# Small matmuls behind the scores of the first half of the first attention, and a shorter emission of the second attention

## The chip, the cores and the metric

The kernel runs on one core of a Trainium2 chip. Its time is the device time of one execution in microseconds; the times shown are those of several runs, and one further execution was recorded by the hardware profiler. TensorE (PE) does the matmuls, VectorE (DVE) and ScalarE (ACT) work on the results, GpSimd (POOL) does a part of the preparation and issues some DMAs, SyncE (SP) issues most DMAs.

## The reference

Four batches of twelve heads of attention over 448 tokens with normalized queries and keys, then two feed-forward layers over all 1792 tokens:

```python
q_n, k_n = (rmsnorm(q, g_q), rmsnorm(k, g_k))          # (4, 12, 448, 64)
scores = scale * np.matmul(q_n, k_n.transpose(0, 1, 3, 2))
attn = np.exp(scores - np.max(scores, axis=-1, keepdims=True))
attn = attn / (np.sum(attn, axis=-1, keepdims=True) + 1e-09)
x = np.matmul(attn, v)                                 # as (1792, 768)
h = x @ w_in                                           # (768, 2048)
y = (h * (1.0 / (1.0 + np.exp(-1.702 * h)))) @ w_out   # (2048, 768)
h = y @ w_in2
out = (np.maximum(h, 0.0) + alpha * np.minimum(h, 0.0)) @ w_out2
```

## The kernel before, in words

**Batches and units.** The work goes batch by batch: the attention of batch b + 1 runs beside the first layer of batch b, and the second layer comes last. A batch has six pairs of heads (NP = 6), and a pair has four units (UNITS): a unit is one set of query columns of both heads, and units 0 and 1 of a pair make up its first half, columns 0 to 256. So unit u belongs to pair u // 4, and batch 0 has the units below 4 * NP = 24.

**The first attention.** Batch 0 is computed in 32-bit floats: scores by two matmuls in the source (four instructions in the profile, line 509), probabilities transposed by TensorE (line 599) and copied by ScalarE (line 604), the sums of exponentials spread by TensorE (line 565), and then the values (line 639). It runs in two passes. `first_pairs` goes through units 0 and 1 of all six pairs, while the words of w_in become 16-bit halves on ScalarE and VectorE (lines 148, 164, 165, 179, 180, 245); three steps of that preparation are emitted per attention step. The second pass goes through units 2 and 3, with the preparation of w_out and the first half of batch 0's hidden units (`first_in`, line 743) beside it. During these stretches POOL loads the values of later batches to scale them (lines 312, 313).

**A unit's scores.** `scores` takes a PSUM tile sp of two banks of 512 columns, of which two buffers exist. It writes columns 0 to 448 of each bank, and VectorE reads the maxima out of them (line 523). `exponent` has ScalarE compute the exponentials out of sp (line 542), after which the buffer is free. `attention` emits, for step i, the scores and exponentials of unit i, the transposes of unit i - 2 (`low`), and the values of the units four steps back (five, from batch 1 on). From batch 1 on the scores are 16-bit matmuls (line 518), and the probabilities are transposed by DMAs on SP's queue (lines 618, 623) before the values.

**The first layer.** For batch 0, `first_moe1` emits the hidden units of columns 256 to 448 in 32 steps (16 blocks, two steps each; line 743, then lines 751 and 752 and the split into halves, lines 140 and 141), and `moe1_out` emits six output columns j in four steps each (line 806, 48 matmuls each, stored by SP, line 815). TICKS = 56 is the sum of both. For the other batches `moe1` takes the place of the hidden part (line 783).

**What sets the order.** Instructions are emitted in program order; a planner with a simulated timeline then orders them on each engine, earlier emitted ones first where several are ready. Every engine works off its queue in that order. At the end of `attention_moe_kernel` the loop over batches emits step i of a batch's first layer, and then as many steps of the next batch's attention as are due by then:

```python
lead = 0 if b else B1_AT
want = first + (last - first) * min(1.0, max(0.0, i + 1 - lead) / (PACE[b] * TICKS - lead))
```

B1_AT = 24 and PACE was 1.0 for all batches. For batch 0 the attention steps 24 to 52, 29 of them, are so spread over 32 steps of the first layer: the last eight steps of the hidden units and the 24 of the output columns. `ones` and `ident` are 128x128 constants of 16 bits (bf16); `tc.issue_after(ins)` orders what is emitted inside it behind `ins` on the same engine.

Of the kernel before, what the change touches and what calls it, by code (L numbers as in the profile page):

```python
# [24 lines left out]
VLAG = 0  # L25
LAG_ = 4
LAG2 = 5
PACE = (1.0, 1.0, 1.0, 1.0)
HOLD = 12800
M_AT = 2  # L30
VS_AT = 8
# [26 lines left out]
def attention_moe_kernel(  # L58
# [17 lines left out]
    nc = tc.nc  # L76
    B, H, S, D = q.shape
# [4 lines left out]
    NP = H // 2  # L82
# [15 lines left out]
    ident = const.tile([128, 128], BF16, name="ident")  # L98
    ones = const.tile([128, 128], BF16, name="ones")
# [395 lines left out]
    def unit(u):  # L495

        P, r = divmod(u, 4)
        return (P, *UNITS[r])

    def scores(u):  # L500
        P, _, _, place = unit(u)
        t1, _ = preps[P]
        sp = ps_s.tile([128, 2, 512], F32, tag="s", name="sp")
        n = 1 if place == 3 else 2
        if u < 4 * NP:
            q0 = (place - 4) * 128 if n == 2 else ST
            for j in range(2):
                ds = slice(64 * j, 64 * j + 64)
                nc.tensor.matmul(
                    out=sp[:, j, 0:S] if n == 2 else sp[ds, 0, 0:S], lhsT=t1[ds, 1, q0:q0 + 64 * n], rhs=t1[ds, 0],  # L510
                    start=True, stop=True
                )
        for i, (e, f) in enumerate(((0, 0), (0, 1), (1, 0)) if u >= 4 * NP else ()):
            kt = t1[:, NT2 * f:NT2 * f + 4].rearrange("p c t -> p (c t)")
            qt = t1[:, NT2 * e + place]
            for j in range(2):
                ds = slice(64 * j, 64 * j + 64)
                nc.tensor.matmul(  # L518
                    out=sp[:, j, 0:S] if n == 2 else sp[ds, 0, 0:S], lhsT=qt[ds] if n == 2 else qt[ds, 64:128], rhs=kt[ds, 0:S],
                    start=(i == 0), stop=(i == 2)  # L520
                )
        nm = small.tile([128, 2], F32, tag="nm", name="nm")
        nc.vector.tensor_reduce(out=nm[:, 0:n], in_=sp[:, 0:n, 0:S], op=ALU.max, axis=AX, negate=True)  # L523
        if u >= 4 * NP:
            nc.scalar.activation(out=nm[:, 0:n], in_=nm[:, 0:n], func=AF.Copy, scale=c_s)  # L525
        probs[u] = (sp, nm, n)
# [151 lines left out]
    def attention(us):  # L678

        LAG = LAG_ if us[0] < 4 * NP else LAG2  # L680
        for i in range(len(us) + LAG):
            if 0 < i <= len(us):
                high(us[i - 1])
            if i < len(us):
                scores(us[i])
                exponent(us[i])
            late = us[0] >= 4 * NP
            for what in (1, 0) if late else (0, 1):
                if what == 0 and 2 <= i <= len(us) + 1:
                    low(us[i - 2])  # L690
                if what and i >= LAG and us[i - LAG] % 2 == 1:
                    values(us[i - LAG] // 4, us[i - LAG] % 4 // 2)
            yield
# [470 lines left out]
    if True:  # L1164
# [80 lines left out]
        for b in range(B):  # L1245
            last = min(NU, 4 * NP * (b + 2)) + LAG2
            first = done
            got = None
            for i, _ in enumerate(moe1(b) if b else first_moe1(g0)):
                lead = 0 if b else B1_AT  # L1250
                want = first + (last - first) * min(1.0, max(0.0, i + 1 - lead) / (PACE[b] * TICKS - lead))
                while done < min(want, NU + LAG2):
# [37 lines left out]
```

## Time and profile before

| what | us |
|---|---|
| median of 3 runs (1151.21 to 1152.9) | 1152.63 |
| the profiled execution | 1150.06 |
| its span, first to last instruction | 1148.2 |
| PE busy | 1059.5 (92%) |
| DVE busy | 803.6 (70%) |
| ACT busy | 680.9 (59%) |
| POOL busy | 177.7 (15%) |
| mean granted clock of TensorE | 0.970 |

The shares are means over stages with different limits, so each stage is to be read by itself. A busy share of TensorE counts matmuls that are being worked on, at whichever clock is granted. The granted clock is a share of full speed: 1.00 is 2.4 GHz and 0.50 is 1.2 GHz, and a value between them says that a stretch had both. A wait names what came last for the instruction that waited.

### The profile page before, as it was taken

How to read it: one execution, taken by the hardware profiler on the slowest of the kernel's cores; microseconds unless marked ns; L12 is line 12 of the kernel's file. 1: busy time of each engine (PE TensorE's matmuls, PEld its weight loads, DVE VectorE, ACT ScalarE, POOL GpSimd, SP SyncE). 2: the span in 40 equal slices, each digit the busy share in tenths (PEclk: the TensorE clock that was granted, in tenths of full speed). 3: DMA queues.
4: the chain of work that ended last, by engine and by line, in shares of the span. 5: the costliest groups of instructions: out<-in, count | busy, mean ns of one | idle time of the engine just before them, and what ended most of it. 6: DMA issues, size and time to landing. Idle time of an engine off the chain costs nothing.

```text
span 1148.2 us, 18347 instructions
## 1 busy us (share of the span) xinstructions
PE 1059.5 (92%) x6752; PEld 580.6 (51%) x6752; DVE 803.6 (70%) x1390; ACT 680.9 (59%) x1396; POOL 177.7 (15%) x364
## 2 busy tenths in 40 slices
PE   3676898897989999999999999999999999999998
PEld 1343566644434555555455455444444477666664
DVE  6988899987869874577533956599977223968341
ACT  4788786878878976688633562356555324645220
POOL 2722003765433242100000000000000000000000
PEclk9687999999989999999999999999999999999999
DMA  7984553478887656555446601665442323363111
GB/s 224 280 212 140 163 153 94 98 165 186 188 164 144 149 135 141 114 118 114 79 117 224 220 1 64 234 219 188 153 157 74 137 70 113 101 188 102 33 30 28
DMA packets 235562, 158.25 MB, mean 138 GB/s; under 512 B 167888, under 2 KB 214736, under 8 KB 235472
## 3 DMA queue, kind: packets, MB, share of 16 engines
q1 hardware_dynamic: 229200, 141.41, 44.4%
q0 software_dynamic: 6272, 15.67, 5.5%
q8 instruction: 53, 0.87, 0.3%
q14 instruction: 37, 0.30, 0.1%
HBM read 92.41 MB, written 25.69 MB: 103 GB/s over the span
## 4 chain that ended last, share of the span: by engine, by line
PE 58%; DVE 14%; DMA 10%; issue 8%; ACT 5%; POOL 4%; SPq 1%; ACTq 0%; DVEq 0%; POOLq 0%
PE op L1072 16%; PE yp L806 14%; PE hp L783 11%; PE h L912 10%; PE xp L639 3%; PE sp L518 2%; DMA pt<-ph 1%; DMA t<-hl 1%; DMA qk<-in_q_dram 1%; DVE ph L611 1%; DMA g<-in_moe_w_out_dram 1%; DMA w2raw<-in_moe_w_in_dram 1%; DVE w2num L165 1%; ACT pr L542 1%; DVE g L141 1%
## 5 line engine op out<-in xcount | busy, mean ns | idle before, releaser
L806 PE MATMUL yp<-g,w1o 128*128 128x448 f16 x1152 | 225.7, 354 | 0.0
L912 PE MATMUL h<-x,w2i 128*128 128x512 f16 (+1 forms) x1152 | 218.9, 352 | 3.1 <-DVE pos L918 1.7
L783 PE MATMUL hp<-x,w1i 128*128 128x448 f16 x864 | 170.4, 354 | 0.9 <-DVE t L792 0.9
L912 PEld LDWEIGHTS <-w2i 128*128 128x128 f16 x1152 | 112.7, 98 | 108.5 <-issue 3.9
L806 PEld LDWEIGHTS <-w1o 128*128 128x128 f16 x1152 | 110.0, 98 | 108.4 <-issue 8.6
L783 PEld LDWEIGHTS <-w1i 128*128 128x128 f16 x864 | 82.0, 98 | 83.4 <-issue 9.8
L523 DVE TENSOR_REDUCE nm<-sp 128x2 f32<-128x896 f32 x96 | 92.7, 966 | 12.6 <-PE sp L518 11.9
L611 DVE SCALAR_TENSOR_TENSOR ph<-pr,sm,ph 128x448 f16<-128x448 f32 x126 | 86.9, 723 | 19.2 <-ACT ph L584 19.1
L917 ACT ACTIVATE pos<-h,sign 128x512 f32<-128x512 f32 (+1 forms) x64 | 40.1, 628 | 86.6 <-PE h L912 80.4
L542 ACT ACTIVATE pr<-sp,nm,c_s 128x448 f32<-128x448 f32 x126 | 90.0, 717 | 2.3 <-DVE ph L611 0.9
L1072 PEld LDWEIGHTS <-even 128*128 128x128 f16 x672 | 65.7, 98 | 43.4
L918 DVE SCALAR_TENSOR_TENSOR pos<-h,slope,pos 128x512 f32<-128x512 f32 (+1 forms) x64 | 43.6, 683 | 60.0 <-ACT pos L917 60.0
L584 ACT ACTIVATE ph<-pr,sm 128x448 f16<-128x448 f32 x126 | 77.5, 658 | 12.3 <-DVE sm L581 11.8
L743 PE MATMUL hp<-x,w1i 128*128 128x256 f16 (+1 forms) x576 | 61.1, 263 | 9.4 <-DVE g L752 7.0
L1072 PEld LDWEIGHTS <-odd 128*128 128x128 f16 x504 | 49.3, 98 | 32.6
L1072 PE MATMUL op<-w2lo,even 128*128 128x384 f16 x384 | 63.4, 326 | 0.0
L743 PEld LDWEIGHTS <-w1i 128*128 128x128 f16 x576 | 52.1, 99 | 20.0 <-issue 16.7
L639 PE MATMUL xp<-pt,vs 128*64 128x256 f16 (+1 forms) x792 | 49.8, 268 | 13.3 <-DMA pt<-ph 12.5
L518 PE MATMUL sp<-t 64*128 64x448 f16 (+1 forms) x432 | 54.2, 357 | 4.1 <-ACT pr L542 4.1
L639 PEld LDWEIGHTS <-vs 128*64 128x64 f16 x792 | 37.8, 112 | 31.7 <-issue 14.1
L525 ACT ACTIVATE nm<-nm,c_s 128x2 f32<-128x2 f32 x72 | 20.8, 289 | 49.8 <-DVE nm L523 49.7
L1072 PE MATMUL op<-w2hi,even 128*128 128x384 f16 x288 | 47.5, 326 | 0.0
(242 smaller groups left out, 1645.1 us busy)
## 6 DMA issues: line engine op xcount, KB each, us to landing
g<-in_moe_w_in_dram SPq DMA_DIRECT2D x24, 512.0 KB, 5.2
g<-in_moe_w_out_dram SPq DMA_DIRECT2D x32, 384.0 KB, 3.7
w2raw<-in_moe_w_in_dram SPq DMA_DIRECT2D x24, 512.0 KB, 5.5
w2raw<-in_moe_w_out_dram SPq DMA_DIRECT2D x16, 768.0 KB, 6.3
g_dram<-pos SPq DMA_DIRECT2D x48, 256.0 KB, 2.0
gp<-g_dram SPq DMA_DIRECT2D x8, 1024.0 KB, 6.7
odd<-g_dram SPq DMA_DIRECT2D x6, 1024.0 KB, 5.4
y_dram<-y SPq DMA_DIRECT2D x24, 224.0 KB, 2.3
```

The source lines that it names most:

```text
L518: nc.tensor.matmul(out=sp[:, j, 0:S] if n == 2 else sp[ds, 0, 0:S], lhsT=qt[ds] if n == 2 else qt[ds, 64:128], rhs=kt[ds, 0:S], start=(i = ...
L523: nc.vector.tensor_reduce(out=nm[:, 0:n], in_=sp[:, 0:n, 0:S], op=ALU.max, axis=AX, negate=True)
L542: nc.scalar.activation(out=pr[i], in_=sp[:, i, 0:S], func=AF.Exp, bias=nm[:, i:i + 1], scale=c_s if u >= 4 * NP else 1.0, accum_out=sm[:, ...
L584: nc.scalar.activation(out=ph[:, i, 0:S], in_=pr[i], func=AF.Copy, scale=sm[:, i:i + 1])
L611: nc.vector.scalar_tensor_tensor(out=ph[:, i, S:2 * S], in0=pr[i], scalar=sm[:, i:i + 1], in1=ph[:, i, 0:S], op0=ALU.mult, op1=ALU.subtract)
L639: nc.tensor.matmul(out=xp[64 * j:64 * j + 64, t:t + n], lhsT=vs[ks, j, c], rhs=pt[ks, 7 * j + kc, 0:n] if b else pt[ks, kc, o:o + n], star ...
L743: nc.tensor.matmul(out=ps, lhsT=w1i[:, kk, e, m * 128:(m + 1) * 128], rhs=xs[0, kk][:, f, cols], start=(i == 0), stop=(i == 3 * KD - 1))
L783: nc.tensor.matmul(out=ps, lhsT=w1i[:, kk, e, m * 128:(m + 1) * 128], rhs=x[:, f], start=(n == 0), stop=(n == 3 * KD - 1))
L806: nc.tensor.matmul(out=ps, lhsT=w1o[:, m, e, j * 128:(j + 1) * 128], rhs=g[:, m, f], start=(n == 0), stop=(n == 3 * KF - 1))
L912: nc.tensor.matmul(out=ps, lhsT=w2i[:, kk, e, m * 128:(m + 1) * 128], rhs=x2[kk][:, f], start=(c == 0), stop=(c == 3 * KD - 1))
L918: nc.vector.scalar_tensor_tensor(out=pos, in0=ps, scalar=slope[:, m:m + 1], in1=pos, op0=ALU.mult, op1=ALU.max)
L1072: nc.tensor.matmul(out=ps, lhsT=ops[:, o, m, f], rhs=rhs[:, e], start=(c == 0), stop=(c == 3 * KH - 1))
```

## The change

Two things change. In `scores`, behind the score matmuls of units with u < 24 and u % 4 < 2 (the first pass of the first attention), 28 matmuls are emitted, each with `ones` as its weights and the first 64 columns of `ident` as its moving operand. They write columns 448 to 512 of the unit's first bank in sp, which nothing reads. They are ordered behind the unit's last score matmul on TensorE, and are emitted ahead of the maxima of line 523. Second, PACE of batch 0 goes from 1.0 to 0.85, so that the 29 attention steps are spread over 0.85 * 56 - 24 = 23.6 steps of batch 0's first layer.

```diff
-PACE = (1.0, 1.0, 1.0, 1.0)
+PACE = (0.85, 1.0, 1.0, 1.0)
@@ -506,7 +506,7 @@
             for j in range(2):
                 ds = slice(64 * j, 64 * j + 64)
-                nc.tensor.matmul(
+                last = nc.tensor.matmul(
                     out=sp[:, j, 0:S] if n == 2 else sp[ds, 0, 0:S], lhsT=t1[ds, 1, q0:q0 + 64 * n], rhs=t1[ds, 0],
                     start=True, stop=True
                 )
@@ -519,6 +519,10 @@
+        if u < 4 * NP and u % 4 < 2:
+            with tc.issue_after(last.ins):
+                for _ in range(28):
+                    nc.tensor.matmul(out=sp[:, 0, S:512], lhsT=ones, rhs=ident[:, 0:512 - S], start=True, stop=True)
         nm = small.tile([128, 2], F32, tag="nm", name="nm")
```

## Rows read from the trace of the kernel before

**Rows 1.** The page, section 2: TensorE's granted clock in 40 slices, in tenths.
```profile
PEclk9687999999989999999999999999999999999999
```

**Rows 2.** Stretches: us, busy us of each engine (instructions), granted clock, DMA share, GB/s.
```profile
20.00:110.00 90.00, 60.96 (x319) 32.31 (x317) 80.92 (x145) 71.37 (x165) 32.20 (x80) 0.73 0.76 213
...
206.00:228.00 22.00, 17.14 (x177) 14.31 (x175) 20.46 (x34) 20.32 (x50) 17.22 (x27) 0.94 0.38 86
228.00:325.00 97.00, 87.21 (x643) 43.09 (x641) 81.05 (x126) 80.43 (x199) 53.81 (x90) 0.98 0.80 175
325.00:338.00 13.00, 7.48 (x62) 3.78 (x61) 4.95 (x10) 8.28 (x21) 2.15 (x4) 0.74 1.00 169
338.00:390.00 52.00, 49.93 (x348) 24.26 (x346) 47.13 (x80) 45.08 (x108) 23.07 (x49) 1.00 0.70 149
390.00:640.00 250.00, 250.00 (x1701) 127.94 (x1698) 152.11 (x254) 160.36 (x363) 27.95 (x59) 1.00 0.55 135
640.00:1148.00 508.00, 499.49 (x2805) 274.18 (x2803) 321.19 (x504) 218.93 (x325) 0.00 (x0) 1.00 0.34 115
```

**Rows 3.** Waits of VectorE, 20 to 110 us: sum us, times, longest.
```profile
DVE g L164 <- ACT g L148: 3.6, 2, 3.0
...
DVE nm L523 <- PE sp L509: 0.6, 1, 0.6
```

**Rows 4.** The chain that ended last, 318 to 345 us: start, us, what.
```profile
325.90 8.11 DMA pt<-ph
```

**Rows 5.** Waits of TensorE, 228 to 338 us.
```profile
PE xp L639 <- DMA pt<-ph: 10.4, 7, 5.1
PE sp L518 <- ACT pr L542: 4.1, 3, 2.4
```

**Rows 6.** TensorE in order of time, 290 to 395 us: start, us, what [idle before].
```profile
323.12 2.07 PE L806 MATMUL yp<-g,w1o 128*128 128x448 f16 x10
...
332.81 0.37 PE L639 MATMUL xp<-pt,vs 128*64 128x192 f16 x1 [5.13 <-DMA pt<-ph]
...
337.30 5.26 PE L783 MATMUL hp<-x,w1i 128*128 128x448 f16 x25
```

**Rows 7.** TensorE in order of time, 180 to 395 us: streams of short matmuls.
```profile
199.90 1.65 PE L743 MATMUL hp<-x,w1i 128*128 128x192 f16 x18 [2.18 <-DVE g L752]
202.01 0.22 PE L120 MATMUL pm<-diag,ones 128*128 128x128 bf16 x1 [0.47 <-DVE diag L118]
202.07 4.62 PE L743 MATMUL hp<-x,w1i 128*128 128x192 f16 x54
...
299.77 1.10 PE L639 MATMUL xp<-pt,vs 128*64 128x192 f16 x22
```

**Rows 8.** Weight loads by line, 195 to 345 us: busy us, mean ns.
```profile
L743 PEld LDWEIGHTS <-w1i 128*128 128x128 f16 x247 | 21.5, 101 | 9.6 <-issue 9.5
```

**Rows 9.** TensorE in order of time, 15 to 125 us: scores, and ones once.
```profile
27.44 1.87 PE L509 MATMUL sp<-w1o 64*128 64x448 f32 x4
...
56.36 1.86 PE L509 MATMUL sp<-w1o 64*128 64x448 f32 x4 [0.55 <-ACT pr L542]
...
63.34 1.02 PE L509 MATMUL sp<-w1o 64*128 64x448 f32 x4
...
82.04 1.87 PE L509 MATMUL sp<-t 64*128 64x448 f32 x4
...
107.44 0.29 PE L120 MATMUL pm<-diag,ones 128*128 128x128 bf16 x1 [5.61 <-DVE diag L118]
```

**Rows 10.** VectorE in order of time, 18 to 120 us: maxima of the scores.
```profile
30.52 1.09 DVE L523 TENSOR_REDUCE nm<-sp 128x2 f32<-128x896 f32 x1
...
58.27 1.09 DVE L523 TENSOR_REDUCE nm<-sp 128x2 f32<-128x896 f32 x1
...
64.53 1.08 DVE L523 TENSOR_REDUCE nm<-sp 128x2 f32<-128x896 f32 x1
...
83.96 1.09 DVE L523 TENSOR_REDUCE nm<-sp 128x2 f32<-128x896 f32 x1
```

## The prediction

> **What bounds the kernel now.** I read the stages first: the granted clock in 40 slices [rows 1] and the busy times by stretch [rows 2]. From 390 us on TensorE is full: 250.00 of 250 us, then 499.49 of 508. What the change does must therefore show before about 338 us, and whatever moves the point at which TensorE becomes full moves the end by as much. Ahead of that point three stretches differ. From 20 to 110 us (the first half of the first attention, with the preparation of both first-layer weights beside it) VectorE is the fullest, 80.92 of 90 us; TensorE works 60.96, so it idles 29.0 us, at a mean granted clock of 0.73: of its two levels, 1.2 and 2.4 GHz, the lower one holds for some half of the time. From 206 to 325 us (the second attention beside the first layer of batch 0) no engine is full: TensorE 87.21, VectorE 81.05, ScalarE 80.43 of 97 us (228 to 325). From 325 to 338 us TensorE works 7.48 of 13 us: the boundary between batch 0 and batch 1.
>
> Next I read who waits. In 20 to 110 us VectorE waits for TensorE hardly at all: 0.6 us for scores, but 3.6 us in the one group of waits for ScalarE [rows 3]. At the boundary the chain is one DMA: a transpose of probabilities takes 8.11 us to land [rows 4], while the DMA engines are at a share of 1.00 [rows 2]. TensorE stands 5.1 us before the values that need it, its longest wait among 10.4 us of that kind and 4.1 us on the exponentials between 228 and 338 us [rows 5], and the solid stream of the next batch starts at 337.30 [rows 6].
>
> **Part 1: the small matmuls, their own cost.** Units with u % 4 < 2 of six pairs: 12 units, 28 matmuls each, 336 in all, each with a load of the 128x128 ones and 64 columns of the identity. No row shows this shape. From below: 18 matmuls of 192 columns end in 1.65 us, and 54 of them in 4.62; one such takes (4.62 - 1.65) / 36 = 82 ns [rows 7], so 64 columns a third, 27 ns, and 28 of them 0.8 us, if loads hide. From above: a 128-wide load takes 101 ns [rows 8]; were the loads strictly one after another, 28 x 101 = 2.8 us. Between these lies a row of short pairs: 22 matmuls with 64-wide loads end in 1.10 us, under 50 ns each [rows 7]; its loads are half as wide. I take 64 ns and 1.8 us for a burst at full clock, near that row; 12 x 1.8 = 21.6 us. That fits into the 29.0 us of idle TensorE in 20 to 110, so as engine time it is hidden by the waits that TensorE has there anyway. At the lower clock a burst costs more: the one bf16 matmul of ones takes 0.22 us at a granted 1.00 [rows 7] and 0.29 us in a stretch at 0.50 [rows 9].
>
> A rule of the Trainium skill speaks against this cost. The full-size rows show loads of 101 ns beside matmuls that follow each other every 82 ns [rows 7, 8], so a load does run beside the matmul ahead of it. "TensorE: Matmul & The Clock Gate", Part 3 (What overlaps and what doesn't), says that a weight load overlaps matmuls in flight only when it is for another row group. By that rule load and matmul would add up, 28 x (101 + 27) = 3.6 us a burst, and with the same share counted as in part 2 the sum would be some 4 us longer, 1153; the rows here decide against it.
>
> **Part 2: who stands behind a burst.** The burst writes columns 448 to 512 of the bank whose columns 0 to 448 the maximum on VectorE (line 523) reads next. The program may order that reduce behind the burst (then it comes up to 1.8 us later) or not (0); I take that it does. What is queued behind it on VectorE is weight preparation, and the exponentials on ScalarE wait for it. Three of the 12 reduces start right at the end of their scores: 56.36 + 1.86 to 58.27, 63.34 + 1.02 to 64.53, 82.04 + 1.87 to 83.96 [rows 9, 10], 0.05 to 0.17 us. The other nine have 1.2 us or more (27.44 + 1.87 to 30.52 is the tightest). With 1.8 us the three come 1.75 + 1.6 + 1.75 us later and the next tightest three 0.6, 0.3 and 0.1: 6.2 us. Part of it ends in waits that VectorE has later anyway (the 3.6 us of [rows 3] are waits for ScalarE), and the queue's order is drawn anew with the burst in it. I take +2 us, bounds 0 and +6.
>
> The transposes and the reciprocals' spreading are queued behind a burst on TensorE too; they have the idle time to catch up in, and I cost them at nothing, or 1.8 us once, at the last pair, if they are late there.
>
> **Part 3: the clock.** Scores take 1.87 us in a cold stretch and 1.02 us in a warm one [rows 9]. If the bursts keep the clock up, the reduces at 58.27 and 83.96, which started 0.05 us behind cold scores, can come 0.85 us earlier each: -1.7 us, less than nothing in cost. All other TensorE work of the stretch ends in waits of TensorE. Bounds: 0 (the clock falls in the gaps as before) and -4 us (all that VectorE waits for ScalarE and TensorE). With part 2 the bursts come to +0.3 us, bounds -4 and +6: by themselves nearly nothing.
>
> **Part 4: the second attention over fewer steps.** The first layer of batch 0 has 56 steps, of which 24 lead. 29 attention steps lay in 32 and now lie in 0.85 x 56 - 24 = 23.6. They end with step 48, that is with the fourth of six output columns (4 steps each). Behind it come two columns of 48 matmuls of 448 columns; 10 such end in 2.07 us [rows 6] and each takes about 0.187 us, so 96 x 0.187 = 18 us of TensorE work that waits for nothing of the attention. Before, TensorE had nothing left at 325 us but the next batch, which waits for the last values. If half of the 18 us lies there, the 5.1 us wait goes, and with it the cold restart: the granted clock in 325 to 338 is 0.74 [rows 2], some 1.5 us on 7.48 of work. That is -6.6 us. The price: a sixth fewer of the 288 output matmuls (48 a column) lie between the attention's steps, so the other 5.3 + 4.1 us of waits [rows 5] have less beside them. I take +2.6 us for that (a quarter of them more), bounds 0 and all of them again, +9.4. VectorE and ScalarE are at 84 and 83% there, against 93 and 92% in 206 to 228 (20.46 and 20.32 of 22 us) [rows 2], so they can follow a faster attention: at 93% the 97 us would be 87, which is the bound on the gain, -10. The DMAs of the next pairs (on POOL's queue) and the transposes (on SP's) issue earlier with their steps; SP also stores the output columns, later now, and nothing waits for these before the second layer. Part 4: -4 us, bounds -9 and +5.
>
> **The sum.** +2 - 1.7 - 4 = -3.7 us. The profiled execution took 1150.06 us (span 1148.2 and 1.9 around it): 1146.4. The median of the runs shown is 2.57 us above it, which gives 1148.9; I say 1149. A difference under 0.2%, 2.3 us, is about what a measurement of this kernel can't tell from none.
>
> **Rivals.**
> *The bursts hold up VectorE (slower).* If a burst takes 3 us, as the lower clock or strictly serial loads would make it, seven of the reduces come later: 2.95 + 2.83 + 2.95 + 1.8 + 1.3 + 1.5 + 0.7 = 14 us; half of that counts, since the waits that swallow delays are used up sooner, and with part 3 at nothing and part 4 at -3 the kernel is 4 us slower, 1156.6. It decides from the point where what reaches VectorE is over some 6 us. For it: VectorE is 90% busy there, and three reduces have no slack. Against: nine have, and TensorE idles 29 us. The rule of the Trainium skill named in part 1 would bring this case about.
> *The faster emission delays the first layer (slower).* By step 32 (the end of the hidden units) some 10 attention steps have been emitted instead of 8. Two more, at about 3.6 us of ScalarE each (80.43 us for some 22 units), stand ahead of the last hidden units' evictions, in 206 to 228 us, where both engines are at 92% and more. Output columns start up to 7 us later; if 4 of that are not made up, and the cover of part 4 is used up for the rest: +3.5 us, 1156.
> *The wait stays (no change).* TensorE's queue is in order. If the last values stand ahead of the 18 us of output columns in it, TensorE waits for the same transpose with work queued behind, as it does already for shorter ones; then part 4 gives 0 and parts 2 and 3 cancel: 1152.6, within 2 us. That the clock doesn't rise is part of this.
>
> **How the numbers follow.** Forecast 0.50 (its own range 1142 to 1150.3); no change 0.20; bursts on VectorE's path 0.22; late first layer 0.08. So faster 0.50, same 0.20, slower 0.30. The likeliest time is 1149. The range takes in the forecast's bounds almost whole (-4 - 9 would be 1140, hardly both at once) and the slower cases but their worst: 1141 to 1160.
>
> **What would show it.** Right: in 20 to 110 us a mean clock near 0.9, VectorE's waits for scores no longer than 3 us in sum, and its stretch ending when it did; output matmuls of batch 0 running where the 5.1 us wait was, and the stream of batch 1 starting 3 to 4 us earlier than 337.30, with TensorE full from about 390 as before. Wrong: the reduces of line 523 waiting for TensorE by over 6 us; bursts of 3 us; the transpose's wait still there with output columns behind it; or a new gap of TensorE between 206 and 230. A change of the stretches behind 390 us would contradict all of it, since nothing there is touched.

## The result, and the profile after

The changed kernel is slower: 1167.77 us median (1159.84 to 1174.96, 6 runs) against 1150.97 (1148.64 to 1152.9, 6 runs) of the kernel before on the same chip, a ratio of 1.013, 95% interval 1.0105 to 1.0155. The forecast was 1149, with a range that ended at 1160. Neither its sign nor its range held.

| what | before | after |
|---|---|---|
| the profiled execution, us | 1150.06 | 1162.19 |
| its span | 1148.2 | 1160.4 |
| PE busy | 1059.5 | 1076.8 |
| DVE busy | 803.6 | 800.8 |
| ACT busy | 680.9 | 682.0 |
| mean granted clock | 0.970 | 0.973 |

Lines below the small matmuls stand four further down in the new listing: the maxima of line 523 are line 527, the exponentials 546, the hidden units of batch 0 line 747, the output columns 810, the hidden units of the other batches 787; the small matmuls are line 525.

The stretches of after, in the columns of [rows 2]:

```profile
20.00:110.00 90.00, 63.26 (x604) 40.65 (x601) 71.19 (x124) 63.60 (x152) 32.36 (x78) 0.84 0.74 205
...
206.00:228.00 22.00, 18.15 (x181) 16.07 (x178) 16.97 (x38) 11.90 (x27) 11.75 (x22) 0.84 0.53 105
228.00:325.00 97.00, 87.33 (x676) 47.33 (x676) 78.75 (x130) 82.30 (x203) 62.63 (x97) 0.96 0.72 152
325.00:338.00 13.00, 12.07 (x90) 6.17 (x91) 8.21 (x13) 6.90 (x18) 3.22 (x7) 1.00 1.10 190
...
640.00:1148.00 508.00, 504.92 (x2829) 276.64 (x2828) 332.51 (x522) 228.13 (x340) 0.00 (x0) 1.00 0.36 122
```

Against [rows 2] the first line already holds a loss of the size measured. The clock of this execution is higher there, 0.84 against 0.73. VectorE, the fullest engine of this stretch, did 71.19 us of work instead of 80.92 and ScalarE 63.60 instead of 71.37: by 110 us VectorE is 9.7 us of work behind. At the boundary (325 to 338) TensorE now works 12.07 us instead of 7.48, but that gives back only a part. Behind it TensorE is full as before and carries the delay to the end.

TensorE's first hidden unit of batch 0 and its first output column, before:

```profile
118.04 0.73 PE L743 MATMUL hp<-x,w1i 128*128 128x256 f16 x4
...
228.13 2.21 PE L806 MATMUL yp<-g,w1o 128*128 128x448 f16 x9
```

and after, 10.2 and 19.5 us later:

```profile
128.25 0.27 PE L747 MATMUL hp<-x,w1i 128*128 128x256 f16 x1 [2.01 <-ACT x L140]
...
247.60 1.67 PE L810 MATMUL yp<-g,w1o 128*128 128x448 f16 x8 [1.75 <-DVE g L756]
```

The small matmuls themselves, TensorE in order of time (a cold burst and two warm ones), and the one maximum that stood behind a burst:

```profile
25.34 1.55 PE L525 MATMUL sp<-ident,ones 128*128 128x64 bf16 x28
28.04 0.99 PE L525 MATMUL sp<-ident,ones 128*128 128x64 bf16 x28
...
101.44 0.99 PE L525 MATMUL sp<-ident,ones 128*128 128x64 bf16 x28
```

```profile
102.47 1.09 DVE L527 TENSOR_REDUCE nm<-sp 128x2 f32<-128x896 f32 x1 [0.58 <-PE sp L525]
```

A burst that runs in one piece costs 0.99 us at full clock ("warm") and 1.55 to 1.68 at the lower one ("cold"), not 1.8, and VectorE waited 0.6 us for all 12 of them together. So the cost is elsewhere. VectorE's waits in 20 to 110 us (sum, times, longest), to be held against [rows 3]:

```profile
DVE a L134 <- DMA row<-line: 6.0, 1, 6.0
DVE w1o L164 <- ACT w1o L148: 5.1, 3, 4.2
DVE w1i L180 <- ACT w1i L179: 3.2, 2, 1.8
...
DVE nm L527 <- PE sp L525: 0.6, 1, 0.6
```

The same stretch of before has, beside the two lines of [rows 3], 0.4 us at line 134 and

```profile
DVE w1o L164 <- ACT w1o L148: 2.9, 2, 2.1
```

None of the first three waits of after is for a small matmul: they are steps of the weight preparation, and a maximum taken over a row that a DMA brings. In the old order the three came to 3.3 us together, now to 14.3. The longest wait but one can be followed through two queues. ScalarE in order of time (first two lines), then VectorE:

```profile
60.09 0.48 ACT L313 ACTIVATE vst<-vst 128x336 f32<-128x336 f32 x1 [5.26 <-DMA vst<-in_v_dram]
...
60.99 0.68 ACT L148 ACTIVATE w1o<-g 128x512 f32<-128x512 f32 x1
```

```profile
57.32 0.14 DVE L106 TENSOR_SCALAR rm_w1i<-rm_w1i 128x1 int32<-128x1 int32 x1
61.70 0.43 DVE L164 TENSOR_SCALAR w1o<-w1o 128x512 int32<-128x512 int32 x1 [4.23 <-ACT w1o L148]
```

ScalarE stands 5.26 us before a load of a later batch's values, whose scores begin past 200 us; the copy of weights queued behind it comes at 60.99, and VectorE stands 4.23 us before that copy. Two in-order queues pass one late load on to the engine that bounds the stretch. "PSUM — Partial Sum Buffer" of the Trainium skill, section "Engine vs sequencer instructions", calls the queues of ScalarE and VectorE strictly first in, first out; these rows agree.

That the order is new can be read off the compiled programs: queue by queue, at least 317 of VectorE's 1390 instructions and 250 of ScalarE's 1203 would have to be moved to get the old sequence back, from VectorE's 29th on. The source adds instructions to TensorE alone.

### The profile page after: what moved, and what is told of

Its sections match the earlier page's. It is cut to its first block, busy times and chain, and to the rows that moved or that the text cites. A ratio compares the mean times of both kernels' runs of the same rounds, so it can differ in the third digit from the quotient of the medians.

```text
span 1160.4 us, 19027 instructions
## 1 busy us (share of the span) xinstructions
PE 1076.8 (93%) x7088; PEld 596.8 (51%) x7088; DVE 800.8 (69%) x1390; ACT 682.0 (59%) x1396; POOL 181.2 (16%) x364
## 4 chain that ended last, share of the span: by engine, by line
PE 57%; DVE 15%; issue 8%; DMA 7%; POOL 7%; ACT 5%; SPq 0%; DVEq 0%; ACTq 0%; POOLq 0%
PE op L1076 16%; PE yp L810 15%; PE h L916 10%; PE hp L787 7%; PE xp L643 3%; PE hp L747 2%; PE sp L518 2%; DMA qk<-in_q_dram 2%; DMA g<-in_moe_w_out_dram 1%; DMA pt<-ph 1%; POOL tn L426 1%; DVE g L141 1%; DMA vst<-in_v_dram 1%; DVE ph L615 1%; DVE ss L416 1%
## 5 line engine op out<-in xcount | busy, mean ns | idle before, releaser
L787 PEld LDWEIGHTS <-w1i 128*128 128x128 f16 x864 | 82.3, 98 | 85.5 <-issue 11.9
L747 PE MATMUL hp<-x,w1i 128*128 128x256 f16 (+1 forms) x576 | 64.0, 272 | 12.3 <-DVE g L756 5.6
L747 PEld LDWEIGHTS <-w1i 128*128 128x128 f16 x576 | 54.4, 103 | 20.9 <-issue 16.3
```

The lines of the kernel that those rows point to most:

```text
L747: nc.tensor.matmul(out=ps, lhsT=w1i[:, kk, e, m * 128:(m + 1) * 128], rhs=xs[0, kk][:, f, cols], start=(i == 0), stop=(i == 3 * KD - 1))
L787: nc.tensor.matmul(out=ps, lhsT=w1i[:, kk, e, m * 128:(m + 1) * 128], rhs=x[:, f], start=(n == 0), stop=(n == 3 * KD - 1))
```

## The experiments

Three theories stood against each other. **A**: the added matmuls make the planner draw a new order for all five queues, and the new order costs the time. **B**: the matmuls themselves, and the waits for them, cost it. **C**: the shorter emission (PACE) costs it. All ratios are against runs of the kernel before on the same chip; they rest on all runs of both kernels, while the times are medians.

| run | us | ratio | 95% interval |
|---|---|---|---|
| pace_only | 1151.78 | 1.0005 | 0.9989 to 1.0021 |
| bursts_only | 1163.68 | 1.0103 | 1.0076 to 1.0130 |
| burst_1 | 1161.64 | 1.0085 | 1.0070 to 1.0101 |
| burst_56 | 1163.83 | 1.0101 | 1.0078 to 1.0124 |
| kept_order | 1154.72 | 1.0022 | 0.9999 to 1.0046 |
| one_u8 | 1174.58 | 1.0217 | 1.0161 to 1.0273 |
| u17_28 | 1162.62 | 1.0091 | 1.0056 to 1.0127 |
| pool_pad | 1189.29 | 1.0322 | 1.0290 to 1.0354 |
| held_bursts | 1154.69 | 1.0026 | 0.9998 to 1.0054 |
| drawn_before | 1164.07 | 1.0102 | 1.0060 to 1.0145 |
| drawn_vst4 | 1162.77 | 1.0077 | 1.0038 to 1.0116 |
| held_vst4 | 1157.04 | 1.0041 | 1.0021 to 1.0061 |
| first_drawn | 1162.30 | 1.0084 | 1.0064 to 1.0104 |
| rest_drawn | 1160.68 | 1.0087 | 1.0064 to 1.0110 |
| drawn_to_50 | 1155.17 | 1.0021 | 0.9997 to 1.0045 |
| drawn_50_118 | 1162.96 | 1.0109 | 1.0080 to 1.0138 |
| drawn_118_228 | 1164.54 | 1.0107 | 1.0061 to 1.0153 |
| drawn_from_228 | 1156.20 | 1.0033 | 1.0006 to 1.0059 |

### One part alone, and the number of matmuls

PACE alone:

```diff
-PACE = (1.0, 1.0, 1.0, 1.0)
+PACE = (0.85, 1.0, 1.0, 1.0)
```

> PACE of batch 0 at 0.85, no small matmuls. The changed kernel came out 17 us slower at the median. Theory A (the bursts redraw the order of ScalarE's and VectorE's queues, and the new order stalls): this run keeps the old order on both, so it is within 3 us of before, 1148 to 1154. Theory B (the bursts' own work and the waits behind them): the same, 1148 to 1154, and if the forecast's part 4 holds, -4 us, 1147. Theory C (the shorter emission costs the time, by thinning out what lies between the attention's steps): 1158 to 1166, with a longer wait of TensorE between 228 and 338 us than the 15.3 us of before.

It changes nothing that these runs resolve, and for a plain reason: on all five queues the compiled program has the same instructions in the same order as before. The planner puts them in the order in which they become ready, and emitting the second attention's steps a little earlier didn't change that. The wait of [rows 6] is still there, TensorE of this run in order of time:

```profile
334.50 0.37 PE L639 MATMUL xp<-pt,vs 128*64 128x192 f16 x1 [5.27 <-DMA pt<-ph]
...
338.81 5.58 PE L783 MATMUL hp<-x,w1i 128*128 128x448 f16 x25
```

The bursts alone, as in the change but with PACE at 1.0 (range 28); then 1 and 56 in each burst:

```diff
+        if u < 4 * NP and u % 4 < 2:
+            with tc.issue_after(last.ins):
+                for _ in range(28):
+                    nc.tensor.matmul(out=sp[:, 0, S:512], lhsT=ones, rhs=ident[:, 0:512 - S], start=True, stop=True)
```

> The 28 matmuls behind the scores of 12 units, PACE at 1.0 as before. Theories A and B: nearly the whole loss, 1160 to 1170, with the first hidden units of batch 0 some 10 us later than at 118 us. Theory C: within 4 us of before.

> One small matmul behind each unit's scores in place of 28 (12 in all, under 1 us of TensorE), PACE at 1.0. Theory A (order): the queues are redrawn all the same, so the time moves by 4 us or more, either way, though the added work is nothing. Theory B (work): within 2 us of before, 1149 to 1153.

> 56 small matmuls behind each unit's scores, PACE at 1.0. Theory B (work and the waits behind it): twice the loss of 28, some +25 to +35 us. Theory A (order): no proportion; anywhere between 0 and +20 us, and not twice the loss of 28. The granted clock in 20 to 110 us should be higher than with 28 in either case (0.84 in the changed kernel).

1, 28 and 56 matmuls in a burst, 12, 336 and 672 in all, lose the same: 0.85, 1.03 and 1.01%. Theory B would have them in proportion. With 56 the clock of 20 to 110 us is 0.93, and the kernel is no faster than with 1, where it is 0.76. In burst_1 the first late step is visible: ScalarE in order of time,

```profile
56.51 0.48 ACT L313 ACTIVATE vst<-vst 128x336 f32<-128x336 f32 x1 [6.98 <-DMA vst<-in_v_dram]
```

where the longest such wait of the kernel before is 3.6 us.

### Fewer matmuls that do or don't redraw the order

kept_order has 117 matmuls, in those units where they leave all but three instructions in their old places. one_u8 has a single matmul in the whole kernel, and u17_28 has 28 behind one unit; both redraw the queues from there on (from VectorE's 99th and 120th instruction). pool_pad has no matmul, but a fill of 448 columns on POOL ahead of the loads of later batches' values; it redraws too. The first two edits below are against the changed kernel with PACE back at 1.0, the last against the kernel before.

```diff
+EXTRA = {21: 28, 20: 28, 16: 28, 5: 28, 4: 1, 12: 2, 17: 2}
 ...
-        if u < 4 * NP and u % 4 < 2:
+        if u in EXTRA:
             with tc.issue_after(last.ins):
-                for _ in range(28):
+                for _ in range(EXTRA[u]):
```

```diff
-        if u < 4 * NP and u % 4 < 2:
+        if u == 8:
             with tc.issue_after(last.ins):
-                for _ in range(28):
+                for _ in range(1):
```

and in u17_28 `u == 17` with the 28 kept;

```diff
+                pad = att_p.tile([128, 448], F32, tag="sq", name="pad", bufs=SQB)
+                with tc.issue_after(rooted[4].ins):
+                    hold = nc.gpsimd.memset(pad, 0.0)
                 for b in range(1, B):
-                    with tc.issue_after(rooted[4].ins):
+                    with tc.issue_after(hold.ins):
```

> Bursts of 28 behind the scores of units 5, 16, 20 and 21 and one or two matmuls behind units 4, 12 and 17 (117 in all, a third of the change's), chosen so that the order of all other instructions on every queue stays that of before but for three that swap with a neighbour. PACE at 1.0. Theory A (the redrawn order costs the time, not the matmuls): within 2 us of before, 1149 to 1154. Theory B (the bursts hold up the reduces and what follows): a third of the loss of 28 in 12 units, +4 us or more, 1155 to 1158.

> One single small matmul in the whole kernel, behind the scores of unit 8; its presence redraws the order of every queue from about 20 us on. Theory A (order): the time moves clearly, by 4 us or more; if before's order is a picked one, upward, some +8 to +12 as with one matmul behind each of 12 units. Theory B (work): no change, within 2 us.

> 28 matmuls behind the scores of unit 17 alone (1 to 1.7 us of TensorE); the order is redrawn from about 50 us on and kept ahead of that. Theory A with the stall of ScalarE at the first load of values (52 us in before) as the main cost: that stall lies ahead of most of the redraw, so the loss is smaller than in the one-matmul run, 0 to +6 us. Theory A with any redraw costing the same: +8 to +12. Theory B: under +2 us.

> No small matmul; a memset of 128x448 on POOL ahead of the loads of later batches' values (about half a us), which redraws the queues from about 35 us on. Theory A (any redraw): the time moves by 4 us or more without any added matmul. Theory B (matmuls): within 2 us of before.

One matmul that redraws the order costs 22.8 us, twice what was expected of it, and u17_28 costs 10.9; 117 that don't redraw it cost 3 or nothing (kept_order came out 0.7 us above what theory A allowed, so it alone decides little). The stretch 20 to 110 us of one_u8:

```profile
20.00:110.00 90.00, 60.54 (x274) 30.57 (x271) 75.00 (x128) 65.78 (x154) 31.05 (x78) 0.67 0.73 205
```

VectorE is 5.9 us of work behind [rows 2] with the clock lower than before. pool_pad is no test of the order: the fill takes 0.47 us, but POOL stood 91.2 us before it could start, POOL in order of time,

```profile
148.21 0.47 POOL L1228 MEMSET pad<- 128x448 f32 x1 [91.22 <-DVE x L662]
148.62 1.34 POOL L312 DMA_DIRECT2D vst<-in_v_dram  x2
```

and the loads of later batches' values start behind it. How much of its 37.5 us is the order's can't be said.

### The order and the matmuls taken apart

The last step separates the two outright. Ordering constraints, which add no instruction, hold every queue to a given sequence of the same instructions (the queues' lists are left out here):

```diff
+def hold_order(tc, bursts):
+    ...
+    for e, text in ORDER.items():
+        ...
+        for x in p:
+            i = by[e][x]
+            if before is not None:
+                tail = bursts.get("after " + before.name)
+                tc.add_manual_dep(i, (tail or before).name, ...)
+            before = i
```

held_bursts is bursts_only with the order of before; drawn_before is the kernel before with the order of bursts_only. Even the semaphore instructions are on each queue as many as in the kernel whose order is held, so the constraints add no work of their own.

> All 336 small matmuls, 28 behind each of the 12 units, PACE at 1.0; and the order of every other instruction on each of the five queues is held to that of the kernel before, by ordering constraints written into the program. So the matmuls are there and the redrawn order is not. Theory A (the loss is the redrawn order; the matmuls themselves cost little): 1152 to 1155 us, a ratio of 1.000 to 1.003, with waits of the maxima for the bursts of 1 to 5 us in sum in 20 to 110 us. Theory B (the matmuls and the waits they make cost it, whatever the order): 1161 to 1164, a ratio of 1.008 to 1.011, as with the order left free. What lies between, 1156 to 1160, would mean that both have a share.

> The kernel before without any of the small matmuls, but with every instruction on each of the five queues held to the order that the planner drew with 28 of them behind each of the 12 units (PACE at 1.0). So the redrawn order is there and the matmuls are not. Theory A (the order): 1160 to 1165 us, a ratio of 1.007 to 1.012, with no small matmul in the kernel, and the first hidden unit at about 123 us instead of 118. Theory B (the matmuls): 1150 to 1153, a ratio within 0.002 of one.

This settles it. All 336 matmuls in the old order cost 0.26% (0 to 0.5); the new order without a single one of them costs 1.02%, as much as bursts_only. held_bursts, stretch and VectorE's waits in 20 to 110 us:

```profile
20.00:110.00 90.00, 65.76 (x631) 39.85 (x628) 78.01 (x138) 69.67 (x164) 31.04 (x78) 0.83 0.73 206
```

```profile
DVE g L164 <- ACT g L148: 4.0, 2, 3.4
DVE nm L529 <- PE sp L525: 3.9, 3, 1.6
```

(line 529 is that of the maxima there), and drawn_before:

```profile
20.00:110.00 90.00, 60.99 (x280) 33.16 (x280) 72.03 (x126) 65.02 (x157) 33.04 (x80) 0.81 0.73 208
```

VectorE is 8.9 us of work behind [rows 2] without any matmul of ones. Even the clock is 0.81, without the matmuls that were to raise it. It differs as much between executions of one order: rest_drawn (below), whose queues are the old ones up to 118 us, has

```profile
20.00:110.00 90.00, 59.95 (x309) 31.48 (x306) 79.07 (x143) 70.31 (x165) 31.66 (x80) 0.86 0.75 208
```

where before has 0.73. At 320 us the same order gives nearly the same trace, with the matmuls (bursts_only) and without (drawn_before):

```profile
320.52 1.39 PE L643 MATMUL xp<-pt,vs 128*64 128x256 f16 x22
...
324.44 0.76 PE L518 MATMUL sp<-t 64*64 64x448 f16 x6 [1.85 <-ACT pr L546]
```

```profile
320.51 1.39 PE L639 MATMUL xp<-pt,vs 128*64 128x256 f16 x22
...
324.45 0.76 PE L518 MATMUL sp<-t 64*64 64x448 f16 x6 [1.87 <-ACT pr L542]
```

### What in the order costs

The waits of ScalarE for later batches' values were the first suspect: 17.3 us in 18 to 125 us of drawn_before, against 13.0 in before. Against it stands that bursts_only, with the order of drawn_before and the same loss, has 11.1. In drawn_vst4 and held_vst4 each of the 24 instructions of line 313 stands four places later in ScalarE's queue (the list of that queue is the edit), in the drawn and in the old order.

> As the run with the redrawn order and no small matmul, but with each of the 24 instructions on ScalarE that take the magnitudes of later batches' values moved four places back in ScalarE's queue, so that what stood behind them no longer waits for their loads. If the blocked queue of ScalarE is what makes the redrawn order dear (11 us of such waits in the trace), those waits go from 11 us to under 3 and the time comes back to 1152 to 1156. If the loss is spread over the order as a whole, the waits go, others take their place, and the time stays at 1159 to 1165.

> The kernel before, without small matmuls, in its own order, but for the 24 instructions on ScalarE that take the magnitudes of later batches' values: each stands four places later in ScalarE's queue. The kernel before has 13 us of waits for their loads in 15 to 260 us. If those waits lie on the path that sets the end, it becomes 2 to 6 us faster, 1146 to 1150. If they lie beside other work there, since the order was drawn around them, nothing changes: 1150 to 1153. If a buffer that comes free later delays the next load by as much, the same.

In the drawn order these waits fell to 9.1 us, not to the 3 expected, and the time to 1.0077, an interval that overlaps that of drawn_before; others took their place (the maximum over the row of line 134 waits 4.1 us instead of 0.7, TensorE's scores 12.6 us for the exponentials instead of 9.1). So these waits are at most a part of it. In the old order the same move makes the kernel 0.41% slower, and these waits are 14.6 us instead of 13.0.

Then the drawn order was put into the old one by stretches, cut where the kernel before starts what it starts at 50, 118 and 228 us; the edit is the list again. first_drawn has all ahead of 118 us in the drawn order, rest_drawn all behind it.

> No small matmul. What the kernel before starts ahead of its first hidden unit (118.0 us: 259 instructions of TensorE, 186 of VectorE, 142 of ScalarE, 112 of POOL, 93 of SP) stands in the order drawn with the matmuls; everything behind it stands in the order of before. If the loss arises in the first pass and is only carried on, the first hidden unit comes at 123 to 127 us and the time is 1159 to 1165, a ratio of 1.007 to 1.012. If it arises behind the first pass, the first hidden unit may be late but later slack takes it back: 1150 to 1155. By the stages of the runs so far (5 to 9 us late at the first hidden unit, 15 to 19 at the last, 10 to 12 at the end) I expect something between: 1155 to 1159.

> No small matmul. The complement: what the kernel before starts ahead of its first hidden unit stands in its own order, and everything behind it in the order drawn with the matmuls. If the loss arises in the first pass, this one is as fast as before: 1150 to 1154, a ratio within 0.002 of one. If it arises behind it, 1158 to 1165, with the first hidden unit at 118 us and the last one past 240. If it is shared, the two runs' losses add up to about the 11 us of the whole order.

> No small matmul. Only what the kernel before starts in its first 50 us (89 instructions of TensorE, 73 of VectorE, 47 of ScalarE, 76 of POOL, 66 of SP) stands in the order drawn with the matmuls; all else in the order of before. If any change of order early costs the whole, because everything behind was laid out for the old arrival times: 1160 to 1163, with the first hidden unit at 122 to 127. If the cost is in proportion to what is moved (of VectorE's queue 19 places of some 374): 1151 to 1154.

> No small matmul. Only what the kernel before starts between 50 and 118 us stands in the order drawn with the matmuls (67 places of VectorE's queue and 47 of ScalarE's are moved); all else in the order of before. Together with the run to 50 us it makes up the run with the first pass redrawn, which lost 10 us. If the loss of the first pass is in the loads and halves of w_in and w_out behind 50 us: 1159 to 1163. If it comes from the first 50 us: 1151 to 1154. If each alone suffices, both are at 1157 or more.

> No small matmul. Only what the kernel before starts between its first and its last hidden unit of batch 0 (118 to 228 us) stands in the order drawn with the matmuls; all else in the order of before. The run with everything behind 118 us redrawn lost 10 us and had its last hidden unit 16 us late. If that is lost here: 1158 to 1163 with the last hidden unit past 240 us. If it is lost behind 228 us: 1151 to 1154.

> No small matmul. Only what the kernel before starts from 228 us on (the output columns of batch 0 beside the second attention, the boundary, and all later batches) stands in the order drawn with the matmuls. TensorE is full from 390 us on in every run so far, so little can be lost there: 1150 to 1154, unless the boundary at 325 to 338 us gets longer, 1154 to 1158. If it is faster than before, the redrawn order hides a gain at the boundary: 1147 to 1150.

The starts of five stages in the traces, us. Only the second and the last stand at the same place of TensorE's queue in both orders (its 700th and 2241st instruction, bursts not counted); in the drawn order the first hidden unit stands 4 places later, the first output column 34 and batch 1's first hidden unit 29 (in after 6 earlier), so these three can come late without anything being late:

| run | first hidden unit | first one of columns 256 to 448 | first output column | batch 1's first hidden unit | batch 1's first output column |
|---|---|---|---|---|---|
| before | 118.0 | 194.6 | 228.1 | 325.0 | 414.0 |
| after | 128.2 | 212.5 | 247.6 | 337.1 | 426.5 |
| held_bursts | 120.9 | 198.0 | 230.9 | 329.1 | 414.6 |
| drawn_before | 126.8 | 209.1 | 248.7 | 345.6 | 424.7 |
| drawn_to_50 | 122.4 | 199.4 | 232.0 | 331.4 | 422.6 |
| drawn_50_118 | 124.1 | 204.0 | 237.2 | 334.3 | 421.8 |
| drawn_118_228 | 124.0 | 206.7 | 238.7 | 336.7 | 426.7 |
| drawn_from_228 | 116.4 | 194.5 | 238.1 | 338.8 | 418.5 |

Two stretches cost as much as the whole, each by itself: 50 to 118 us 1.09%, and 118 to 228 us 1.07%. So do the two halves, first_drawn with 0.84% and rest_drawn with 0.87%, where a loss shared between them was expected to add up. The first 50 us cost 0.2% or nothing in the times (its one profiled execution is slower than that), and what lies behind 228 us 0.3%. In the stretch from 50 on the bounding engine waits for ScalarE; VectorE's waits in 50 to 128 us, before and then drawn_50_118:

```profile
DVE w1o L164 <- ACT w1o L148: 3.9, 4, 2.1
DVE g L164 <- ACT g L148: 3.6, 2, 3.0
```

```profile
DVE w1o L164 <- ACT w1o L148: 11.4, 5, 6.3
DVE w1i L180 <- ACT w1i L179: 3.6, 2, 2.0
DVE a L134 <- DMA row<-line: 1.9, 1, 1.9
```

From 118 on ScalarE stands longer before the hidden units; its longest group of waits in 118 to 250 us, before and then drawn_118_228:

```profile
ACT t L751 <- PE hp L743: 5.9, 9, 1.2
```

```profile
ACT t L751 <- PE hp L743: 11.7, 10, 3.3
```

There one displaced step can be followed. VectorE's step on `last_t` (line 752) is what TensorE's first hidden unit of columns 256 to 448 waits for. In before it ran ahead of a maximum of the weight preparation (line 245) and of a step on queries and keys (line 437) that waits for POOL; in the drawn order it stands behind both. VectorE and then TensorE, before:

```profile
194.11 0.43 DVE L752 SCALAR_TENSOR_TENSOR last_t<-t,hp 128x256 f32<-128x256 f32 x1
194.59 3.13 PE L743 MATMUL hp<-x,w1i 128*128 128x192 f16 x36 [0.16 <-DVE last_t L752]
```

and drawn_118_228:

```profile
203.31 2.09 DVE L437 TENSOR_TENSOR qk<-qk,rs 128x896 f32<-128x896 f32 x2 [1.69 <-POOL rs L427]
205.32 0.95 DVE L245 TENSOR_REDUCE rm_w1o<-num1o 128x1 f32<-128x768 f32 x1
206.19 0.41 DVE L752 SCALAR_TENSOR_TENSOR last_t<-t,hp 128x256 f32<-128x256 f32 x1
206.65 7.26 PE L743 MATMUL hp<-x,w1i 128*128 128x192 f16 x54 [3.83 <-DVE last_t L752]
```

The wait of 3.83 us is in after, bursts_only, drawn_before and rest_drawn too; in held_bursts, first_drawn and the other three pieces it is 0.15 or 0.16. What putting this one step back would give was not tried.

The losses of the pieces don't add up: 1.09 and 1.07%, and 1.02% with both and the rest. By the two starts that can be compared, drawn_to_50 is 4.8 us late and then 8.6, drawn_50_118 9.4 and 7.8, drawn_118_228 12.1 and 12.7, and drawn_before, with all of it, 14.5 and 10.7. A kernel with one stretch drawn has an order that no planner drew, with seams of its own; so the pieces show that a displaced stretch costs time, and not which share of the whole loss it has. Why each alone already reaches some 10 us, and which single displaced instruction would be enough, stays open.

## Why the prediction was wrong, step by step

**What bounds the kernel** held: from 390 us on TensorE is full in every run (at least 247 of 250 us, then 499 of 508), and a delay ahead of it moves the end. What was missing is that VectorE's 80.92 of 90 us in 20 to 110 belong to the old order of the work: with the drawn one they are 72 (drawn_before).

**Part 1, the burst.** Taken 1.8 us at full clock; measured 0.99, and 1.55 to 1.68 cold, 16.0 us for all 336 instead of 21.6. The lower bound (0.8) was the nearer one. The rule of the Trainium skill in "TensorE: Matmul & The Clock Gate", Part 3 (What overlaps and what doesn't), that a load overlaps matmuls in flight only when it is for another row group, is decided against once more: the 336 loads take 111 ns each on the mean, which one after another would be 3.1 us a burst.

**Part 2, who stands behind a burst.** In the old order (held_bursts) this was sized well: three maxima wait, 3.9 us in sum where 5.1 us were worked out for three of them (the sum for all six, given as 6.2, is 6.1), and the kernel is 3.0 us slower (0.26%; -0.2 to 6.2) where +2 with bounds 0 and +6 stood, +0.3 together with part 3. **This part has the failed step all the same**: "the queue's order is drawn anew with the burst in it. I take +2 us, bounds 0 and +6." The redraw was named and then costed as if it could only move the waits for the burst. By itself it costs 11.7 us (drawn_before, 1.02% of 1151; 6.9 to 16.7), some four times what the matmuls do at the middle of both intervals, and it reaches four other queues and hundreds of instructions.

**Part 3, the clock.** It was 0.84 where "near 0.9" stood, and 0.93 with 56 in a burst. That the 28 raised it isn't shown: five kernels without a small matmul and with the old order up to 110 us have 0.73 (before, drawn_118_228), 0.75, 0.76 and 0.86 (rest_drawn). Nor did it bring anything that can be measured: held_bursts has 0.83 and isn't faster. The -4 us that bounds this part was also misread: VectorE waits for ScalarE in two groups in 20 to 110 us, 3.6 and 2.9 us, not in one. The sum doesn't use that bound.

**Part 4, the emission.** -4 us was taken; alone it is +0.6 (-1.3 to +2.4), that is nothing, since no instruction changes its place. The step that failed is that an emission order was taken for a queue's order, when the kernel's own description says that a planner orders by readiness. Nor did it put output columns behind the last values: in after, as in before, all 288 matmuls of them stand ahead of the last pair's values in TensorE's queue. The wait of 5.1 us does go in after, but by another order. TensorE in order of time:

```profile
333.30 3.96 PE L810 MATMUL yp<-g,w1o 128*128 128x448 f16 x20
337.09 0.35 PE L787 MATMUL hp<-x,w1i 128*128 128x448 f16 x1
339.36 0.74 PE L518 MATMUL sp<-t 64*128 64x448 f16 x6 [1.91 <-ACT pr L546]
...
343.46 1.30 PE L518 MATMUL sp<-t 64*128 64x448 f16 x6 [1.41 <-ACT pr L546]
...
345.05 5.70 PE L787 MATMUL hp<-x,w1i 128*128 128x448 f16 x23
350.68 0.27 PE L643 MATMUL xp<-pt,vs 128*64 128x192 f16 x1
```

Ahead of the values that waited in [rows 6] (350.68 here, without a wait) stand 23 matmuls of batch 1's hidden units, and TensorE waits 1.91 and 1.41 us for exponentials before them; the stream starts at 345.05, not before 337.30. In bursts_only and drawn_before, where PACE is 1.0, the wait before these values shrinks to 1.9 and 2.7 us. Whether PACE does something in the redrawn order (after 1.013, bursts_only 1.0103, intervals that overlap) isn't resolved. The price of part 4 is put there at a quarter of 9.4 us and taken as 2.6; a quarter is 2.4. Its bounds, -9 and +5, aren't worked out.

**The rivals.** "The wait stays" was right for the emission by itself. "The bursts hold up VectorE" had the right side, and its mechanism is real in held_bursts, but at 3.9 us it stays below the 6 us from which it was to decide; its 1156.6 was not the result, and what made after slow wasn't it. "The faster emission delays the first layer" had the right side too, and output columns did start 19.5 us late; but they start 17.9 us late in bursts_only, where the emission is the old one, and 1.9 in pace_only, which has the faster one. No rival was the one that happened: the planner's answer to the added instructions.

**What was to show it.** The signs did their work. The maxima waited 0.6 us, not over 6, so VectorE's path through the bursts was ruled out by one row; "VectorE's stretch ending when it did" failed by 10 us, and that pointed at the queues.

## What to carry to other kernels

Where a planner orders the queues, an edit is two changes: the instructions and the new order of all others. Compare the compiled order queue by queue first; if it moved, price the edit with the old order held. Seven kernels here with a redrawn order lost 0.85 to 2.2%, whether 672 matmuls had caused it, or one, or none were in them (drawn_before); none gained, but why the old order is the better one no run shows. And in a stretch that TensorE doesn't bound, no run here got time back from a higher clock of it.

## What was not expected of the hardware

Weight loads of 128x128 that follow each other closely overlap one another in the records, not only the matmuls. The loads of line 525 in 15 to 110 us of after (count, busy us, mean ns of one, idle before):

```profile
L525 PEld LDWEIGHTS <-ones 128*128 128x128 bf16 x336 | 13.8, 111 | 11.1 <-issue 10.7
```

336 loads of 111 ns are 37.3 us in sum, but cover 13.8 us. A pair of load and 64-column matmul ends every 35 ns (0.99 us / 28) at full clock and every 55 to 60 ns (1.55 to 1.68 us / 28) in the cold bursts.
